# A new order of 594 steps, with other engines, buffers and held stores, for a fused attention and adapter kernel

## The chip, the core and the metric

The kernel runs on one core of a Trainium2 chip. The time is that of the device, in microseconds; a lower one is better. The core has five engines that work side by side, each through its own instructions in a fixed order: TensorE (PE, matrix products; PEld is its loading of weights), VectorE (DVE), ScalarE (ACT), GpSimd (POOL) and SyncE (SP). An instruction that needs another engine's result, or a buffer that another engine still uses, waits on a semaphore, and all that is queued behind it on its engine waits too. Transfers between HBM and the core's memory are issued here by POOL and SP, and run on 16 DMA engines.

## What is computed

Two layers, one after the other. The first is an attention without softmax (8 batches, 8 heads, 576 positions, 64 values per head), the second a mixture of two out of eight small adapters on each of the 4608 rows:

```python
q_p, k_p = phi(q, cos_w, sin_w), phi(k, cos_w, sin_w)   # relu(x) * cos, relu(x) * sin
kv = np.einsum('bhsf,bhsd->bhfd', k_p, v)
z = np.sum(k_p, axis=2)
num = np.einsum('bhsf,bhfd->bhsd', q_p, kv)
den = np.einsum('bhsf,bhf->bhs', q_p, z)[..., None] + 1e-06
x = num / den                                           # rows of 512
logits = x @ w_gate
# for the two largest logits of a row: softmax weight w, expert e
delta += w * ((x @ A[e]) @ B[e])
out = x + delta
```

## The kernel before

**Batches and groups.** Each batch's 576 positions lie as 64 partitions times 9 columns j. K, V and Q of a batch are loaded by POOL, which also casts them to bf16 on the way (lines 399, 401 and 419; the first K halves come through SP, line 410, into two output buffers). For each batch K goes through a ReLU (lines 432 on ACT, 434 on DVE) and V is scaled by the cosine and the sine of the position: on DVE as one product for four or two heads' pairs (line 446), on ACT as nine activations, one for each j (line 444). PE forms the state of a batch in 72 or 2 x 36 small matmuls (line 457, "kv"), which DVE or ACT copies into a block matrix BD (lines 469 and 471).

The output rows are made in 36 groups of 128 rows. Groups of kind "one" take two columns of one batch, groups of kind "two" take one column of two batches; the last nine groups all need batches 6 and 7. For a group PE transposes Q (line 541), ACT applies the ReLU (line 547), DVE multiplies by the tangent (line 567), PE multiplies with the state (line 585, "num"), and DVE takes the reciprocal of the denominator (line 596) and the quotient, xt (line 601). PE transposes xt (line 610), ACT or DVE copies it (xT, lines 245 and 247), and PE multiplies with the adapters' A and the gate together (line 623, "za").

Router steps go by 13 keys of three groups each (the last two of two and one): two largest logits, their sum, difference, mask, sigmoid, weights and weighted z (lines 637 to 672), a transpose on PE (line 681) and its copy (zgT). The output of a group is the product with B, with or without xt added on PE through the identity (lines 692 and 694, "dx"), then either a copy by ACT (line 245) or an addition of xt by DVE (line 704) into an output buffer, osb. Each key's three groups share one of seven osb buffers, which are written out by SP or POOL (lines 714 and 717).

**What sets the order.** Every step is declared with `pl.add`: its engine or alternatives, what it needs and makes, the buffers that it uses. Three tables at the top of the file, made outside of it by a search, then decide: `ORDER` is the one order in which all 594 steps are issued, and so the order on each engine; `CHOICE` says which alternative (engine) a step takes; `SLOTS` which buffer each use of a pool gets. In `Plan.run` nothing is computed any more, the tables are checked and the steps returned in order. Semaphores follow from the data and the buffers.

Two short tables are beside them. `HOLD` maps a store to another issue that has to come first: the store then waits for that issue, on its own queue. `FILL` puts a number of matmuls without use (line 318, 252 columns each) ahead of a step on PE, whose result is overwritten.

```python
            if s.idx in fill:
                pe_fill(fill[s.idx], s)
            issued[s.idx] = s.emit()
            if s.idx in hold:
                tc.add_manual_dep(issued[s.idx].ins, issued[hold[s.idx]].ins.name,
```

At the start DVE clears four BD matrices (line 331) and sets a matrix of ones, warm (line 299), on which PE runs 2 x 18 wide matmuls (line 305) while loads arrive; POOL makes a ramp TVi (line 257), ACT its sine and cosine TVf (lines 260 and 261, the second with the constant halfpi as bias), and DVE and PE spread the tangents into TT by way of the identity (lines 271, 275, 282 and 289).

Of the kernel before, what the change touches and what calls it, by code (L numbers as in the profile page):

```python
# [17 lines left out]


ORDER = [  # L20
    26, 0, 1, 19, 27, 29, 17, 20, 14, 45, 2, 16, 9, 23, 15, 13, 36, 10, 32, 11, 12, 28, 33, 18, 3, 37, 31, 4, 46, 51,
    7, 21, 8, 48, 30, 52, 38, 50, 39, 49, 35, 44, 41, 34, 115, 61, 114, 5, 62, 40, 116, 42, 22, 6, 43, 117, 118, 55,
    60, 121, 54, 70, 125, 122, 124, 119, 120, 126, 135, 71, 123, 145, 134, 127, 144, 136, 298, 154, 69, 131, 53, 137,
    299, 128, 132, 300, 79, 146, 129, 130, 155, 147, 57, 47, 156, 301, 133, 56, 80, 65, 302, 58, 59, 303, 138, 64,
    141, 78, 170, 171, 139, 142, 140, 161, 172, 160, 143, 24, 148, 162, 25, 305, 304, 149, 151, 173, 306, 355, 163,
    373, 152, 356, 150, 63, 88, 153, 307, 157, 357, 360, 358, 374, 308, 158, 375, 359, 159, 309, 66, 378, 361, 73, 89,
    310, 68, 67, 362, 74, 363, 167, 164, 87, 364, 181, 168, 165, 180, 376, 166, 190, 377, 182, 191, 169, 311, 174,
    312, 183, 313, 177, 175, 379, 97, 192, 176, 393, 178, 72, 314, 200, 315, 394, 75, 193, 201, 395, 398, 396, 179,
    412, 397, 96, 76, 380, 77, 316, 399, 83, 381, 82, 187, 184, 188, 400, 107, 185, 413, 206, 186, 207, 417, 189, 194,
    317, 202, 208, 414, 197, 195, 415, 196, 416, 106, 81, 382, 216, 217, 318, 369, 98, 209, 84, 198, 218, 418, 419,  # L30
    365, 370, 219, 387, 86, 199, 320, 366, 385, 105, 92, 85, 383, 386, 210, 384, 91, 319, 203, 388, 321, 322, 401,
    204, 211, 226, 390, 205, 227, 402, 430, 212, 228, 323, 431, 213, 324, 229, 236, 237, 435, 432, 214, 403, 433, 238,
    90, 392, 223, 215, 367, 404, 405, 239, 434, 368, 420, 93, 436, 224, 421, 437, 406, 101, 372, 326, 94, 325, 407,
    95, 450, 100, 327, 220, 408, 246, 221, 422, 451, 247, 410, 222, 424, 423, 438, 225, 230, 439, 99, 329, 328, 442,
    455, 452, 330, 248, 102, 453, 231, 425, 411, 443, 232, 454, 469, 103, 456, 457, 104, 440, 233, 470, 441, 444, 426,
    234, 474, 471, 445, 447, 235, 249, 427, 472, 458, 110, 332, 473, 459, 331, 240, 333, 464, 475, 241, 250, 476, 460,
    465, 242, 273, 429, 272, 461, 292, 109, 274, 462, 253, 252, 243, 254, 463, 477, 409, 275, 282, 478, 283, 468, 467,
    244, 263, 293, 255, 334, 466, 284, 262, 245, 487, 251, 264, 335, 481, 488, 371, 108, 336, 448, 337, 489, 265, 111,
    428, 338, 490, 492, 449, 285, 491, 482, 483, 493, 113, 294, 479, 494, 507, 112, 480, 484, 495, 256, 508, 496, 486,
    485, 509, 512, 259, 257, 510, 258, 511, 499, 501, 513, 260, 514, 500, 266, 261, 502, 497, 339, 267, 506, 515, 268,  # L40
    340, 516, 269, 505, 498, 341, 342, 517, 270, 504, 343, 276, 271, 526, 277, 518, 279, 278, 344, 521, 446, 280, 527,
    345, 281, 286, 346, 391, 531, 528, 347, 529, 287, 289, 288, 530, 348, 519, 532, 503, 522, 290, 543, 533, 520, 525,
    291, 534, 295, 523, 544, 535, 524, 349, 545, 389, 548, 546, 351, 350, 547, 536, 352, 549, 296, 540, 550, 537, 560,
    297, 541, 538, 561, 551, 562, 353, 565, 539, 552, 563, 354, 555, 564, 542, 566, 553, 567, 557, 556, 554, 568, 579,
    558, 569, 570, 580, 571, 559, 581, 589, 584, 582, 574, 573, 583, 575, 572, 585, 586, 576, 577, 587, 588, 578, 590,
    591, 592, 593,
]
CHOICE = [
    0, 0, 0, 0, 0, 0, 0, 0, 0, 0, 0, 0, 0, 0, 0, 0, 0, 0, 0, 0, 0, 0, 0, 0, 0, 0, 0, 0, 0, 0, 0, 0, 0, 0, 0, 0, 0, 0,
    0, 0, 0, 0, 1, 0, 0, 0, 0, 1, 1, 1, 0, 0, 0, 1, 0, 0, 0, 0, 0, 0, 0, 0, 0, 1, 0, 0, 0, 0, 0, 0, 0, 0, 0, 0, 0, 0,  # L50
    0, 0, 0, 0, 0, 0, 1, 0, 0, 0, 0, 0, 0, 0, 0, 0, 0, 0, 0, 0, 0, 0, 0, 0, 0, 0, 0, 0, 0, 0, 0, 0, 0, 0, 0, 0, 0, 0,
    0, 0, 0, 0, 0, 0, 0, 0, 0, 0, 0, 0, 0, 0, 0, 0, 0, 0, 0, 0, 0, 0, 0, 0, 0, 0, 0, 0, 0, 0, 0, 0, 0, 0, 0, 0, 0, 0,
    0, 0, 0, 0, 0, 0, 0, 0, 0, 0, 0, 0, 0, 0, 0, 0, 0, 0, 0, 0, 0, 0, 0, 0, 0, 0, 0, 0, 0, 0, 0, 0, 0, 0, 0, 0, 0, 0,
    0, 0, 0, 0, 0, 0, 0, 0, 0, 0, 0, 0, 0, 0, 0, 0, 0, 0, 0, 0, 0, 0, 0, 0, 0, 0, 0, 0, 0, 0, 0, 0, 0, 0, 0, 0, 0, 0,
    0, 0, 0, 0, 0, 0, 0, 0, 0, 0, 0, 0, 0, 0, 0, 0, 0, 0, 0, 0, 0, 0, 0, 0, 0, 0, 0, 0, 0, 0, 0, 0, 0, 0, 0, 0, 0, 0,
    0, 0, 0, 0, 0, 0, 0, 0, 0, 0, 0, 0, 0, 0, 0, 0, 0, 0, 0, 0, 0, 0, 0, 0, 0, 0, 0, 0, 0, 0, 0, 0, 0, 0, 1, 0, 0, 1,
    0, 0, 0, 0, 0, 0, 0, 0, 0, 0, 0, 0, 0, 0, 0, 0, 0, 0, 0, 0, 0, 0, 0, 0, 0, 0, 0, 0, 0, 0, 0, 0, 0, 0, 0, 0, 0, 0,
    0, 1, 0, 0, 0, 0, 0, 0, 1, 0, 0, 0, 1, 0, 0, 0, 0, 0, 0, 0, 0, 0, 1, 0, 0, 0, 0, 0, 0, 0, 1, 0, 0, 0, 0, 0, 0, 0,
    0, 0, 0, 0, 0, 0, 0, 0, 0, 0, 1, 0, 1, 0, 0, 0, 0, 0, 0, 0, 0, 0, 0, 0, 0, 0, 0, 0, 0, 0, 1, 1, 0, 0, 0, 0, 0, 0,
    0, 0, 0, 0, 0, 0, 1, 1, 0, 0, 0, 1, 0, 0, 0, 0, 0, 0, 0, 0, 0, 0, 1, 1, 0, 0, 0, 0, 0, 1, 0, 0, 0, 0, 0, 0, 0, 0,  # L60
    0, 0, 0, 0, 0, 0, 1, 1, 0, 0, 0, 0, 1, 0, 0, 0, 0, 0, 0, 0, 0, 0, 0, 1, 1, 0, 0, 0, 0, 0, 1, 0, 0, 0, 0, 0, 0, 0,
    0, 0, 0, 1, 1, 0, 0, 0, 0, 0, 1, 0, 0, 0, 0, 0, 0, 0, 0, 0, 0, 0, 0, 1, 1, 0, 0, 0, 0, 0, 1, 1, 0, 0, 0, 0, 0, 0,
    0, 0, 0, 0, 0, 0, 0, 0, 0, 0, 0, 0, 0, 0, 0, 0, 0, 0, 0, 0, 1, 1, 1, 0, 0, 0, 0, 0, 0, 0, 0, 0, 0, 0, 0, 0, 0, 1,
    0, 0, 0, 0, 0, 0, 0, 0, 0, 0, 0, 0, 0, 0, 0, 0, 0, 0, 1, 0, 0, 1, 1, 0,
]
SLOTS = [
    0, 1, 0, 2, 0, 1, 0, 1, 0, 1, 0, 0, 1, 0, 1, 0, 0, 1, 2, 2, 2, 2, 0, 2, 3, 3, 3, 1, 0, 3, 0, 1, 4, 0, 0, 0, 1, 0,
    0, 2, 0, 1, 2, 2, 2, 1, 1, 2, 3, 3, 1, 0, 0, 3, 3, 0, 1, 1, 0, 0, 0, 1, 1, 1, 0, 1, 2, 1, 2, 3, 2, 2, 1, 0, 4, 0,
    1, 5, 3, 3, 1, 2, 6, 0, 0, 7, 1, 4, 1, 1, 8, 3, 1, 0, 0, 9, 1, 2, 10, 0, 0, 0, 1, 11, 1, 0, 12, 2, 2, 0, 1, 13, 1,
    2, 14, 3, 3, 0, 0, 15, 1, 1, 2, 3, 4, 0, 2, 0, 1, 1, 1, 0, 4, 0, 1, 3, 1, 0, 0, 0, 5, 1, 2, 6, 2, 2, 0, 1, 1, 0,  # L70
    0, 7, 3, 3, 0, 2, 8, 0, 0, 9, 3, 4, 1, 1, 10, 2, 2, 1, 2, 13, 0, 0, 12, 2, 3, 1, 1, 14, 0, 2, 11, 3, 1, 1, 0, 0,
    0, 1, 15, 1, 4, 1, 2, 2, 0, 0, 3, 0, 0, 1, 1, 4, 0, 0, 2, 1, 1, 2, 3, 3, 1, 0, 2, 1, 3, 2, 1, 3, 0, 0, 0, 1, 0, 2,
    3, 0, 3, 3, 2, 1, 1, 0, 3, 2, 1, 1, 2, 3, 0, 0, 1, 2, 0, 1, 2, 0, 0, 0, 3, 0, 3, 2, 0, 0, 0, 1, 1, 1, 0, 1, 3, 3,
    0, 2, 1, 0, 0, 0, 3, 1, 2, 4, 3, 2, 2, 1, 1, 1, 2, 0, 0, 5, 2, 1, 1, 0, 0, 0, 3, 1, 2, 6, 3, 3, 1, 1, 1, 1, 2, 1,
    2, 0, 1, 1, 0, 0, 0, 0, 3, 0, 2, 1, 1, 3, 0, 1, 1, 1, 0, 1, 0, 4, 2, 3, 1, 0, 0, 0, 2, 0, 2, 2, 1, 3, 0, 1, 1, 1,
    3, 1, 3, 0, 2, 0, 2, 0, 0, 0, 3, 0, 2, 5, 3, 0, 1, 1, 1, 1, 1, 1, 2, 1, 0, 3, 0, 0, 0, 2, 0, 1, 6,
]

HOLD = [
    (371, 392), (409, 98), (446, 486), (503, 504),  # L80
]

FILL = [
    (7, 2), (118, 13), (135, 2), (56, 2), (138, 8),
]


# [780 lines left out]
```

## Time and profile before

| | us |
|---|---|
| three runs: median (lowest to highest) | 108.25 (108.07 to 109.98) |
| the profiled execution: its own time | 108.82 |
| its span, first to last instruction | 106.7 |

The busy time of an engine is the sum over its instructions, whatever they wait for in between. The page's groups show the costliest work:

| line | engine, what | count | busy us, mean ns |
|---|---|---|---|
| L585 | PE, num | 384 | 22.6, 223 |
| L601 | DVE, quotient xt | 36 | 24.0, 683 |
| L446 | DVE, V scaling | 17 | 18.9, 1138 |
| L547 | ACT, ReLU of transposed Q | 20 | 18.4, 944 |
| L245 | ACT, copies into osb | 29 | 15.6, 567 |
| L245 | ACT, copies into xT | 16 | 14.9, 941 |
| L567 | DVE, tangent product | 20 | 12.3, 624 |
| L444 | ACT, V scaling, one j each | 27 | 9.1, 425 |

Loads come in at a steady rate: in the trace each load of 1.2 MB (576 KB as bf16) lands 2.8 to 2.9 us after the one before, and the last, K of batch 7, at 73.4 us. SP's first store is issued at 72.79 us; POOL's first at 55.42, behind the loads on the same queue. How matmuls overlap with one another is modelled in the profile, so that "PE busy" is not PE at its peak, and an idle engine costs nothing where another one sets the end.

### The profile page before, as it was taken

What the parts mean: (1) busy time and instruction counts of PE and PEld (TensorE: products, weight loads), DVE (VectorE), ACT (ScalarE), POOL (GpSimd) and SP (SyncE); (2) the same over time, 40 slices, a digit from 0 to 9 for tenths busy, and PEclk for the clock granted to TensorE, in tenths of its full rate; (3) what the DMA queues carried; (4) which work ended last, traced back from release to release, by engine and by line L of the source; (5) the groups of instructions that cost most, each with busy time, mean ns of one, the idle gap of its engine ahead of it and who ended that gap; (6) DMA issues with size and microseconds to landing.
All of it is one profiled execution on the core that took longest, in us unless ns stands there. A gap on an engine that the chain in (4) does not pass through costs nothing.

```text
span 106.7 us, 4019 instructions
## 1 busy us (share of the span) xinstructions
PE 90.9 (85%) x1693; PEld 66.7 (63%) x1704; DVE 89.9 (84%) x254; ACT 77.8 (73%) x139; POOL 33.3 (31%) x53
## 2 busy tenths in 40 slices
PE   4978999959788599976999999998979969998920
PEld 1334468847687589864768686874868657775300
DVE  5973819897999999999798998997999969989940
ACT  7406982996388749999999998968999732677620
POOL 6999965522402222226321121221200202040000
PEclk9999999999999999999999999999999999999995
DMA  2999999999999999999999999999999998888993
GB/s 79 357 179 204 192 198 207 207 210 194 203 208 209 206 208 208 208 207 210 206 213 203 207 213 203 207 208 285 395 331 269 220 292 266 274 217 256 381 390 131
DMA packets 18321, 24.70 MB, mean 231 GB/s; under 512 B 4256, under 2 KB 15648, under 8 KB 18304
## 3 DMA queue, kind: packets, MB, share of 16 engines
q0 software_dynamic: 15984, 16.98, 88.5%
q1 hardware_dynamic: 2320, 7.47, 21.2%
q8 instruction: 13, 0.21, 0.7%
q14 instruction: 4, 0.03, 0.1%
HBM read 28.85 MB, written 9.44 MB: 359 GB/s over the span
## 4 chain that ended last, share of the span: by engine, by line
PE 44%; DVE 27%; ACT 12%; issue 7%; POOL 5%; DVEq 0%; POOLq 0%
PE pnd L585 13%; DVE xt L601 7%; PE ps L610 6%; PE ps L623 5%; PE pnd L457 5%; DVE VV L446 4%; PE ps L305 4%; ACT VV L444 3%; PE ps L692 3%; PE ps L541 3%; ACT BD L469 3%; ACT qTcs L547 2%; DVE osb L704 2%; PE ps L694 2%; DVE qTcs L567 2%
## 5 line engine op out<-in xcount | busy, mean ns | idle before, releaser
L585 PE MATMUL pnd<-BD,qTcs 128*128 128x130 bf16 (+1 forms) x384 | 22.6, 223 | 2.7 <-issue 1.3
L601 DVE TENSOR_TENSOR xt<-pnd,rden 128x512 bf16<-128x512 f32 x36 | 24.0, 683 | 0.1
L585 PEld LDWEIGHTS <-qTcs 128*128 128x128 bf16 (+1 forms) x384 | 18.3, 103 | 6.1 <-issue 4.2
L547 ACT ACTIVATE qTcs<-ps 128x1024 bf16<-128x1024 bf16 (+1 forms) x20 | 18.4, 944 | 3.9 <-PE ps L541 3.7
L446 DVE TENSOR_TENSOR VV<-Vb,TV 128x2304 bf16<-128x2304 bf16 (+1 forms) x17 | 18.9, 1138 | 2.6 <-DMA Vb<-in_v_dram 2.6
L245 ACT COPY osb<-ps 128x512 f32<-128x512 f32 (+1 forms) x29 | 15.6, 567 | 3.8 <-DVE osb L247 1.5
L245 ACT COPY xT<-ps 128x1024 bf16<-128x1024 bf16 (+1 forms) x16 | 14.9, 941 | 4.5 <-PE ps L610 4.4
L610 PE MATMUL ps<-ident,xt 128*128 128x128 bf16 x144 | 13.5, 222 | 0.8 <-DVE xt L601 0.4
L567 DVE TENSOR_TENSOR qTcs<-qTcs,TT 128x1024 bf16<-128x1024 bf16 (+1 forms) x20 | 12.3, 624 | 1.2 <-ACT qTcs L547 1.2
L717 POOL DMA_DIRECT2D out_dram<-osb x9 | 4.9, 540 | 25.3 <-DVE ps L655 6.8
L541 PE MATMUL ps<-ident,Qb 128*64 128x128 bf16 x288 | 11.1, 221 | 1.5 <-ACT qTcs L547 1.0
L457 PE MATMUL pnd<-VV,Kb 64*64 64x130 bf16 x576 | 10.3, 218 | 1.6 <-DVE xt L601 1.2
L610 PEld LDWEIGHTS <-xt 128*128 128x128 bf16 x144 | 9.8, 115 | 3.1 <-DVE xt L601 0.8
L457 PEld LDWEIGHTS <-Kb 64*64 64x64 bf16 x576 | 8.8, 106 | 4.3 <-issue 2.3
L692 PE MATMUL ps<-xt,ident 128*128 128x512 bf16 x29 | 10.9, 381 | 0.6 <-DVE zgT L247 0.3
L305 PE MATMUL ps<-warm 128*128 128x512 bf16 x36 | 9.8, 435 | 1.5 <-DVE warm L299 1.5
L541 PEld LDWEIGHTS <-Qb 128*64 128x64 bf16 x288 | 8.7, 109 | 3.7 <-issue 2.3
L623 PE MATMUL ps<-AW,xT 128*128 128x136 bf16 x144 | 10.5, 223 | 0.1
L469 ACT CAST BD<-pnd 64x520 bf16<-64x520 f32 x15 | 9.0, 598 | 2.1 <-PE pnd L457 1.2
L623 PEld LDWEIGHTS <-xT 128*128 128x128 bf16 x144 | 9.0, 98 | 1.5
L694 PE MATMUL ps<-Ball,zgT 128*128 128x512 bf16 x25 | 9.2, 380 | 0.6 <-DVE zgT L247 0.6
L444 ACT ACTIVATE VV<-Vb,TVf 128x128 bf16<-128x128 bf16 (+1 forms) x27 | 9.1, 425 | 0.0
(63 smaller groups left out, 117.3 us busy)
## 6 DMA issues: line engine op xcount, KB each, us to landing
Vb<-in_v_dram POOLq DMA_DIRECT2D x6, 576.0 KB, 20.0
Qb<-in_q_dram POOLq DMA_DIRECT2D x6, 576.0 KB, 20.1
Kb<-in_k_dram POOLq DMA_DIRECT2D x6, 576.0 KB, 20.1
out_dram<-osb SPq DMA_DIRECT2D x10, 256.0 KB, 5.9
out_dram<-osb POOLq DMA_DIRECT2D x6, 256.0 KB, 10.1
out_dram<-osb SPq DMA_DIRECT2D x2, 768.0 KB, 3.4
osb<-in_k_dram SPq DMA_DIRECT2D x2, 576.0 KB, 4.1
Vb<-in_v_dram POOLq DMA_DIRECT2D x4, 288.0 KB, 6.7
```

What stands on the lines that cost most here:

```text
L245: nc.scalar.copy(o, i)
L305: nc.tensor.matmul(out=pF(up), lhsT=warm[:, 0:128], rhs=warm, start=True, stop=True)
L446: nc.vector.tensor_tensor(out=o, in0=i, in1=TV[:, cs].unsqueeze(1).to_broadcast([128, n, J, D]), op=ALU.mult)
L457: nc.tensor.matmul(out=pt[64 * hh:64 * hh + 64, par, a * 2 * W:(a + 1) * 2 * W], lhsT=kt[r, 2 * a + hh, j, :], rhs=vt[r, 2 * a + hh, j, :] ...
L541: nc.tensor.transpose(out=pt[64 * hh:64 * hh + 64, n, 2 * a:2 * a + 2, x], in_=qt[:, c, j, :], identity=ident)
L547: nc.scalar.activation(tQT[S_(uqt)][:, 0, 0:n], pB(up)[:, 0:n], AF.Relu)
L567: nc.vector.tensor_tensor(out=v[1], in0=v[0], in1=f4, op=ALU.mult)
L585: nc.tensor.matmul(out=nd[r, a, 0:4 * W].rearrange("p (h e w) -> p h e w", h=2, e=2)[:, :, par], lhsT=st, rhs=bd[:, par, a, cs].rearrange( ...
L601: nc.vector.tensor_tensor(out=tXT[S_(uxt)].rearrange("p (a h d) -> p a h d", a=2, h=4), in0=nd_view(und)[:, :, :, 0:D], in1=tRD[S_(urd)].u ...
L610: nc.tensor.transpose(out=pB(up)[:, lo:lo + 128], in_=tXT[S_(uxt)].rearrange("p (x c) -> p c x", c=4)[:, c], identity=ident)
L623: nc.tensor.matmul(out=pF(uza)[:, n * AW_W:(n + 1) * AW_W], lhsT=tXTT[S_(u)][:, k, c, :], rhs=AW[:, c, :], start=(c == 0), stop=(c == 3))
L692: nc.tensor.matmul(out=pF(udx), lhsT=ident, rhs=tXT[S_(uxt)], start=True, stop=False)
```

## The change

Only the five tables change. No step is added or dropped except fillers, and no function is touched.

- `ORDER`: almost every step has another place; neighbours on an engine mostly keep close to one another.
- `CHOICE`: 31 steps change. From DVE to ACT: V scaling of a half of batch 0 (the sine), of a half of batch 1 and of all of batch 2 (cosine), the copy of A and the gate (AW), zgT of keys 0 and 11, two output additions of "dx", two one-group copies of xT, two of the half-row copies at the end, and one half of batch 0's state. From ACT to DVE: V scaling of a half of batch 1, one K half's ReLU of batch 1, the halves of the states of batches 0 and 7, one two-group and one one-group copy of xT, zgT of key 3, one output addition. With an output copy that goes to ACT, PE adds xt through the identity, and with one that goes to DVE it doesn't. Five stores go from POOL to SP and two from SP to POOL.
- `SLOTS`: other buffers, for osb among others: keys 7 to 12 used buffers 4, 2, 0, 5, 1, 6 and now use 5, 1, 6, 2, 5, 3.
- `HOLD`: five stores wait for another issue instead of four.
- `FILL`: 24 fillers instead of 27, in other places.

On POOL's queue a load of Q (three columns of batch 0) and one of V now stand ahead of the ramp, the second half of V of batch 1 two places earlier, and V of batch 7 ahead of Q of batches 6 and 7. On DVE the four clears of BD and the warm matrix now stand ahead of halfpi.

```diff
--- before.py
+++ after.py
@@ -18,70 +18,70 @@
 ORDER = [
-    26, 0, 1, 19, 27, 29, 17, 20, 14, 45, 2, 16, 9, 23, 15, 13, 36, 10, 32, 11, 12, 28, 33, 18, 3, 37, 31, 4, 46, 51,
...
-    591, 592, 593,
+    26, 15, 31, 27, 14, 45, 19, 16, 20, 1, 17, 29, 0, 2, 36, 9, 3, 32, 11, 13, 33, 28, 10, 18, 51, 37, 30, 12, 4, 46,
...
+    592, 593,
 ]
...
 HOLD = [
-    (371, 392), (409, 98), (446, 486), (503, 504),
+    (371, 372), (390, 486), (391, 447), (429, 107), (467, 506),
 ]
 
 FILL = [
-    (7, 2), (118, 13), (135, 2), (56, 2), (138, 8),
+    (118, 7), (134, 2), (138, 7), (304, 8),
 ]
```

The numbers are those of the steps. In `HOLD` 371, 390, 391, 429 and 467 are stores by SP of keys 0, 1, 1, 3 and 5; 372, 486, 447 and 506 are stores by POOL of keys 0, 6, 4 and 7, and 107 is the load of Q of batch 7.

## The prediction

> **What bounds the kernel now.** I read the page's busy row first, then the windows cut at the starts of the state matmuls (kv, L457), then the chain of waits, then the DMA answers.
>
> ```profile
> PE 90.9 (85%) x1693; PEld 66.7 (63%) x1704; DVE 89.9 (84%) x254; ACT 77.8 (73%) x139; POOL 33.3 (31%) x53
> ```
>
> No engine alone fills the span of 106.7 us. The windows say where each is full (stretch, length, busy time of each engine, granted TensorE clock, DMA share, GB/s):
>
> ```profile
> 0.00:20.00 20.00, 17.59 (x209) 9.84 (x209) 13.51 (x30) 11.71 (x29) 15.93 (x27) 1.00 1.13 202
> 20.00:34.30 14.30, 11.86 (x248) 10.01 (x242) 12.81 (x35) 10.88 (x12) 4.31 (x7) 1.00 1.28 205
> 34.30:60.80 26.50, 23.39 (x530) 18.97 (x531) 25.31 (x69) 23.89 (x41) 7.58 (x10) 1.00 1.21 208
> 60.80:80.00 19.20, 17.94 (x382) 13.80 (x388) 17.99 (x50) 17.19 (x30) 3.31 (x6) 1.00 1.15 261
> 80.00:104.00 24.00, 20.12 (x340) 14.08 (x345) 20.31 (x75) 14.10 (x31) 2.19 (x4) 1.00 0.90 285
> ```
>
> The columns are PE, PEld, DVE, ACT, POOL. From 34.3 to 60.8 us DVE is busy 25.31 of 26.50: this middle is DVE's. Before it, DVE has 7.98 us of idle time (20 - 13.51 and 14.3 - 12.81); from 80 to 104 both DVE and PE have nearly 4 us. The cuts at 34.3, 60.8 and 80 are the starts of the state matmuls of batches 2, 5 and 7, "kv2", "kv5", "kv7" below.
>
> Loads do not bind. In the trace the K loads of batches 2, 5 and 7 land at 30.0, 56.3 and 73.4 us, 4.3, 4.5 and 6.5 us before their kv starts (of which the ReLU takes 0.75 on DVE or 2.1 on ACT).
>
> The chain of waits, in order of time, from kv7 on (start, length, what):
>
> ```profile
> 79.94 1.25 PE pnd L457 x69
> ...
> 84.84 0.53 PE pnd L585 x14
> 85.37 0.96 issue
> 86.33 0.25 PE pnd L585 x2
> ...
> 95.20 0.36 PE ps L610 x4
> ...
> 95.59 0.42 DVE xT L247
> ...
> 100.60 0.44 DVE osb L247
> ...
> 101.74 0.14 DVE osb L247
> ...
> 102.78 0.44 DVE osb L247
> 103.23 0.37 ACT osb L245
> ```
>
> From 79.94 to 95.6 the chain is PE, with one hole of 0.96 us in which PE waits for nothing the profile shows. From 95.6 it is a DVE-led ladder of router steps and copies. The hole is instruction fetch, as I read it:
>
> ```profile
> PEld L585 <- issue: 4.2, 9, 1.1
> ...
> q8 instruction: 13, 0.21, 0.7%
> ```
>
> Queue q8 moved 13 blocks of 16 KB, each in 0.9 to 1.0 us; the one from 84.52 to 85.44 ends inside the hole, the one from 72.26 to 73.20 lies by another (0.34 at 72.32). The chain's issue pieces after 70 us that are worth counting are 0.34, 0.18, 0.96, 0.15 and 0.28: 1.9 us.
>
> **The change, part by part.** Every step's computation is kept. I count each stage's steps in both orders and price them with rows: halves of V scaling 0.70 on DVE, 2.68 on ACT (9 of the 18 that took 5.36); a whole one 1.31 (half of 2.62) or 3.65; xt 0.60 and rden 0.12 back to back; state copy 0.69 on DVE, 0.60 on ACT; K ReLU 0.75, 2.1, halves 1.17 on ACT and about 0.4 on DVE (estimate: half of 0.75); two-group copy of xT 0.66 or 1.0, one-group 0.42 or 0.59; output copy 0.65 or 0.55, halves 0.42 or 0.37; sig 0.22, zgT 0.35 or 0.48. Small router steps and PE steps are alike in both orders.
>
> - Up to kv2: one half and one whole V scaling, and the copy of the adapter weights (0.28 + 0.17 on DVE, about 0.8 on ACT), go from DVE to ACT; a K half goes back, as does one xT copy. DVE -1.3, ACT +5.0, PE +0.2.
> - kv2 to kv5: DVE -0.1, ACT 0, PE -0.2, though within it kv4 stands later on PE, behind six output products (dx) where it was behind one.
> - kv5 to kv7: two more qT products on DVE, one residual add fewer; five more output copies on ACT. DVE +0.8, ACT 0, PE +0.5.
> - After kv7: DVE does 4 output copies where it did 7, one tan product, one xT and one zgT copy fewer. DVE -2.1, ACT +1.7, PE -0.4.
>
> Now what reaches the end. **To kv2** ACT decides. Walked by rows, ACT's work from its first table copy at 8.82 to the end of batch 2's ReLU is 0.21 + 3 x 2.68 + 0.57 + 6 x 1.0 + 0.6 + 1.17 + 3 x 0.6 + 3.65 + 0.8 + 2.1 = 24.9, so 33.8 without a gap; back-to-back pieces overlap by about 0.07 each, which gives near 33.0, against 33.93 now. Inputs are there in time: the second half of V of batch 1 is moved ahead of two loads on POOL's queue and lands near 14 instead of 15.57; V2, landed at 23.51, stays in place. At the start POOL issues a Q and a V load (0.92 + 0.72) before the ramp, so TVf comes 1.6 later, but it is then behind DVE's five memsets (four of 0.54, one of 0.48) and needs halfpi, now last of them; the tangent matmul waits for the identity, 7.44 now, 0.2 later then. I take 0 to there and -0.4 at kv2. **kv2 to kv5** 0. **kv5 to kv7**: DVE's +0.8 falls into a stretch with 1.2 us of DVE idle (19.2 - 17.99); I take +0.3. **After kv7** PE's -0.4 counts, since PE is the chain to 95.6; of the fetch hole of 0.96 I take half, -0.5; on the last ladder one 256-column copy (0.42) and one zgT copy leave DVE, and the last two copies run on ACT one behind the other, where now DVE's 0.44 is followed by ACT's 0.37: -0.7. Sum: -0.4 + 0 + 0.3 - 0.4 - 0.5 - 0.7 = -1.7.
>
> **Stores.** Three stores go from POOL to SP (SP 19 to 22, POOL 12 to 9). POOL's are cheap to drop: it idles up to 6.8 us for them. On SP one issue takes 1.16 us at the median, so its queue is 3.5 us longer; its last store before the final four goes at 94.9, the first of the four at 98.2, so 3.3 us of cover. The last needs only its own data; cost 0, at most 0.3. Every output buffer was followed to its next writer: the nearest is the buffer of router group 3, whose second store now stands fourth on SP (about 76, landed by 82) before group 7 writes it near 85. Cover 3 us; price if late, the lateness. The holds order stores behind other issues on one queue or the other and hold no engine but SP.
>
> **Fillers** fall from 27 to 24 matmuls of 0.12 (1.57 for 13). The granted clock is 1.00 in every window above. The Trainium skill, "TensorE: Matmul & The Clock Gate" (Why this matters for your kernels), speaks against fewer: a gap of some 3 us sends the clock back to half. By it one such window, 3.4 us at half speed, would cost 1.7 us. But from 20.0 to 34.3 PE idles 2.44 in all and the fillers there (10 x 0.12 = 1.2) would make 3.6, spread over 14 us; the longest single PE gap is 1.2. I take 0.
>
> A second rule of the skill speaks against the change's worth: "Runtime: NRT & Kernel Launch" (Instruction fetch mechanics), has the cost of a new 16 KB block "mostly hidden". By it the holes are not fetch and the store order buys nothing: the sum would be -1.2. By the row it is -1.7, and the bound of what fetch can give is the 1.9 above; that it costs more with SP's longer queue bounds it below, about +1.0 (one more such hole). I stay with the trace, at half of the one hole.
>
> **Rivals.**
> - *Nothing arrives.* DVE's relief after kv7 turns into DVE waiting for PE, which is the chain there and loses 0.4; the fetch hole moves. For it: PE 20.12 of 24 against DVE 20.31, so PE stays. Sum +0.3 - 0.4 - 0.2 = -0.3: median 108.0.
> - *All of it arrives.* DVE's -1.3 before kv2 and -2.1 after kv7 count whole, with 1.5 of the 1.9 of fetch: -1.3 + 0.3 - 2.1 - 1.5 = -4.6: 103.7. Against it: ACT ties the first, PE the second.
> - *ACT becomes the bound before kv2*, slower. ACT now has gaps of 0.80, 1.76, 0.82, 1.92 and 0.52 between 8.82 and 33.93, 5.8 in all. If 4 of them come back beside the 5.0 of new work, kv2 starts at 38.3, and the DVE-bound middle has 1.2 us of slack to take it in: +4.0, less the 1.6 after kv7: +2.4, median 110.7. It decides from kv2 near 38 on. Against it: the old gaps waited for qT transposes and state matmuls that now stand as early or earlier.
> - *It doesn't do what it says*: fetch holes as many as before. That is the first rival's -0.3, or my sum without its -0.5, 107.05.
>
> **The numbers.** The sum is against the profiled execution, 108.82 (span 106.7 and 2.1 around it): 107.1. The three timed runs have median 108.25, 0.57 less: 106.5. The forecast (105.4 to 107.4) has 0.42, nothing arrives (107.4 to 109) 0.23, all arrives 0.15, ACT 0.20. 2% is 2.17 us, about what a measurement of this kernel can tell from no change (its runs spread over 1.9). Faster by over 2% is below 106.1: two fifths of the forecast, 0.17, and all of the second, 0.15: 0.32. Slower is ACT's 0.20; the rest 0.48. Range: 104.2 leaves out half of the case of -4.6, 110.7 half of ACT's.
>
> **What would show it.** kv2 at 33.5 to 34.3 (right) or over 37 (ACT rival); kv7 within 1 us of 79.9; DVE busy near 87 and ACT near 84; from kv7 to the last copy 22 us where it is 23.7 now; issue pieces on the chain after 70 us near 1.4. I am wrong if PE waits on a store, if a Q transpose waits for ACT in the first 34 us, or if PE's clock falls below 1.00 before 100 us.

## The result, and the profile after

| | before | after |
|---|---|---|
| median, lowest to highest, us | 108.16 (108.03 to 109.98, 4 runs) | 106.66 (106.36 to 106.86, 4 runs) |
| profiled execution, its span | 108.82, 106.72 | 106.86, 105.09 |

The ratio is 0.986, interval 0.983 to 0.990: 1.4% less time, inside the 2% that count as no change, and 0.2 us from the predicted 106.5. Executions over 1.5% above the fastest of the same kernel are left out of all ratios here; most of the kernels have some, and the one without fillers has four of ten, at 109.4 to 109.8 us and a mean granted clock of 0.961 to 0.964.

The busy row of the changed kernel, first part of the page:

```profile
PE 91.4 (87%) x1692; PEld 67.0 (64%) x1702; DVE 89.2 (85%) x248; ACT 82.9 (79%) x161; POOL 31.1 (30%) x50
```

ACT took over 5.1 us of work, DVE shed only 0.7, and PE grew by 0.5: none of the three that fill the stages got shorter by what the kernel gained. So the time is again read by stages. The windows of the changed kernel, cut at its own kv2, kv5, kv7 and just short of the end of the copies at 100.88 (stretch, length, then PE, PEld, DVE, ACT, POOL, granted clock, DMA share, GB/s):

```profile
0.00:20.00 20.00, 17.40 (x193) 9.11 (x194) 13.27 (x28) 12.97 (x33) 15.80 (x27) 1.00 1.15 205
20.00:34.46 14.46, 12.70 (x260) 10.81 (x260) 13.88 (x37) 14.18 (x27) 4.25 (x6) 1.00 1.28 204
34.46:60.34 25.88, 23.28 (x537) 19.10 (x539) 25.16 (x69) 23.19 (x42) 7.26 (x10) 1.00 1.21 208
60.34:79.24 18.90, 18.00 (x361) 13.73 (x363) 18.76 (x51) 16.94 (x31) 1.64 (x3) 1.00 1.16 268
79.24:100.70 21.46, 20.00 (x348) 14.23 (x350) 18.16 (x68) 15.39 (x34) 2.17 (x4) 1.00 0.91 287
```

ACT is now full ahead of kv2, 14.18 of 14.46, and DVE full from 60.34 to 79.24, 18.76 of 18.90. The stages themselves, from the instructions' own times (the last packet is the last piece of a store to move):

| stage, us | before | after | difference |
|---|---|---|---|
| start to kv2 | 34.32 | 34.46 | +0.14 |
| kv2 to kv5 | 26.47 | 25.88 | -0.59 |
| kv5 to kv7 | 19.15 | 18.90 | -0.25 |
| kv7 to end of last output copy | 23.67 | 21.64 | -2.03 |
| last copy to last packet | 1.65 | 2.96 | +1.31 |
| last packet to end of span | 1.46 | 1.25 | -0.21 |

These make -1.63; another -0.33 lies outside the span. Two rows carry the story: the last stage gained two microseconds, and then the stores took 1.3 back.

One execution is not the kernel, and the first row shows it. Six other profiles of the changed order, in kernels that leave the work ahead of kv2 as it is (one but for its fillers), have kv2 at 33.90, 33.90, 33.91, 33.98, 34.24 and 34.72 us; four of the old order with its choices have it at 34.30 to 34.36. In the changed order kv2 follows ACT's first table copy (TT) by 24.82 or 24.83 us each time; what varies is that copy, from 9.06 to 9.89. It waits for PE, which runs through its first 18 warming matmuls before. These take 0.63 us each at first and 0.38 later, and that turn came at 7.7 us in the profile above and at 5.1 in that of the stores put back (below). The granted clock stands at 1.00 all the while, so the row doesn't say why.

The chain of waits of the changed kernel in its last stage, from kv7 on (start, length, what):

```profile
79.31 1.18 PE pnd L457 x69
...
84.20 0.59 PE pnd L585 x16
84.79 0.35 PE ps L610 x4
85.14 0.17 PE ps L681 x3
85.31 0.60 PE pnd L585 x16
...
93.23 3.92 DMA out_dram<-osb
97.15 0.67 DVE osb L704
...
99.12 0.41 DVE osb L247
99.53 0.23 DVE zgT L247
99.76 0.05 issue
99.81 0.40 PE ps L694
100.23 0.37 ACT osb L245
100.61 0.27 ACTq L863
```

The 0.96 us of "issue" that stood at 85.37 has no successor. The ladder at the end is shorter by the DVE copy that ACT now takes. And there is a new line: a store of 3.92 us ahead of a DVE addition at 97.15, into the buffer that this store has just written out. It is no wait. DVE's own timeline has no gap there:

```profile
96.80 0.42 DVE L672 TENSOR_TENSOR zg<-ps,w 128x256 bf16<-128x256 f32 x1
97.14 0.68 DVE L704 TENSOR_TENSOR osb<-ps,xt 128x512 f32<-128x512 f32 x1
```

The chain goes back to the last event that a step could have waited for, and the landing of the store came as DVE got free. In the profile without holds the same addition comes as early, counted from kv7 (17.9 us in both), with no store in its chain.

### The profile page after: what moved, and what is told of

It is laid out like the page before. It is cut to its first block, busy times and chain, and to the rows that moved or that the text cites. A ratio compares the mean times of both kernels' runs of the same rounds, so it can differ in the third digit from the quotient of the medians.

```text
span 105.1 us, 4032 instructions
## 1 busy us (share of the span) xinstructions
PE 91.4 (87%) x1692; PEld 67.0 (64%) x1702; DVE 89.2 (85%) x248; ACT 82.9 (79%) x161; POOL 31.1 (30%) x50
## 4 chain that ended last, share of the span: by engine, by line
PE 46%; ACT 21%; DVE 18%; issue 5%; DMA 4%; ACTq 0%; SPq 0%; DVEq 0%
PE pnd L585 13%; PE ps L305 10%; ACT qTcs L547 7%; PE pnd L457 6%; PE ps L610 5%; ACT BD L469 4%; PE ps L541 4%; DVE xt L601 4%; DMA out_dram<-osb 4%; PE ps L623 3%; ACT Kb L432 3%; ACT VV L444 2%; ACT xT L245 2%; DVE VV L446 2%; ACT osb L245 2%
## 5 line engine op out<-in xcount | busy, mean ns | idle before, releaser
L585 PE MATMUL pnd<-BD,qTcs 128*64 128x130 bf16 (+1 forms) x384 | 22.5, 222 | 2.5 <-ACT BD L469 1.7
L585 PEld LDWEIGHTS <-qTcs 128*64 128x64 bf16 (+1 forms) x384 | 18.2, 103 | 5.7 <-issue 3.0
L446 DVE TENSOR_TENSOR VV<-Vb,TV 128x2304 bf16<-128x2304 bf16 (+1 forms) x15 | 17.0, 1155 | 3.3 <-DMA Vb<-in_v_dram 3.3
L245 ACT COPY osb<-ps 128x512 f32<-128x512 f32 (+1 forms) x32 | 16.5, 564 | 2.1 <-PE ps L694 1.0
L444 ACT ACTIVATE VV<-Vb,TVf 128x128 bf16<-128x128 bf16 (+1 forms) x45 | 15.5, 432 | 0.0
L305 PE MATMUL ps<-warm 128*128 128x512 bf16 x36 | 10.7, 467 | 2.6 <-DVE warm L299 2.6
L541 PE MATMUL ps<-ident,Qb 128*64 128x128 bf16 x288 | 11.7, 222 | 0.8 <-issue 0.7
L717 POOL DMA_DIRECT2D out_dram<-osb x7 | 3.8, 537 | 26.4 <-ACT sig L662 10.7
L469 ACT CAST BD<-pnd 64x520 bf16<-64x520 f32 x14 | 8.4, 600 | 1.9 <-DVE BD L471 1.6
```

Source lines behind the costliest of these rows:

```text
L245: nc.scalar.copy(o, i)
L305: nc.tensor.matmul(out=pF(up), lhsT=warm[:, 0:128], rhs=warm, start=True, stop=True)
L444: nc.scalar.activation(o[:, :, j], i[:, :, j], AF.Copy, scale=TVf[:, cs, j:j + 1])
L446: nc.vector.tensor_tensor(out=o, in0=i, in1=TV[:, cs].unsqueeze(1).to_broadcast([128, n, J, D]), op=ALU.mult)
L469: nc.scalar.copy(o, i)
L541: nc.tensor.transpose(out=pt[64 * hh:64 * hh + 64, n, 2 * a:2 * a + 2, x], in_=qt[:, c, j, :], identity=ident)
```

## Experiments

### The choices without the order, and the order without the choices

The kernel before with only the changed `CHOICE`:

```diff
 CHOICE = [
-    0, 0, 0, 0, 0, 0, 0, 0, 0, 0, 0, 0, 0, 0, 0, 0, 0, 0, 0, 0, 0, 0, 0, 0, 0, 0, 0, 0, 0, 0, 0, 0, 0, 0, 0, 0, 0, 0,
+    0, 0, 0, 0, 0, 0, 0, 0, 0, 0, 0, 0, 0, 0, 0, 0, 0, 0, 0, 0, 0, 0, 0, 0, 0, 1, 0, 0, 0, 0, 0, 0, 0, 0, 0, 0, 0, 0,
...
```

> The kernel before with the new engine choices only (order, buffers, holds and fillers as before). If the gain is the relief of VectorE, which the choices make, it is here: ratio to before 0.986 to 0.990. If order and choices only pay together, since ScalarE's extra 5 us ahead of batch 2's state matmul then stand where nothing was cleared for them: 1.00 to 1.02, with that matmul starting after 36 us instead of 34.3.

Measured: 112.2 us, ratio 1.037 (1.033 to 1.041), worse than either case expected. kv2 starts at 39.01. The timeline of this kernel on ACT (start, length, what, tiles; in brackets the idle time before it and what ended it):

```profile
27.46 1.21 ACT L469 CAST BD<-pnd 64x520 bf16<-64x520 f32 x2 [1.82 <-PE pnd L457]
28.70 3.70 ACT L444 ACTIVATE VV<-Vb,TVf 128x256 bf16<-128x256 bf16 x9
32.42 1.94 ACT L547 ACTIVATE qTcs<-ps 128x1024 bf16<-128x1024 bf16 x2
34.25 0.62 ACT L245 COPY AW<-Ald 128x512 bf16<-128x512 bf16 x1
34.76 0.23 ACT L245 COPY AW<-Gld 128x32 bf16<-128x32 bf16 x1
34.88 2.13 ACT L432 ACTIVATE Kb<-Kb 128x2304 bf16<-128x2304 bf16 x1
```

From 27.46 to 37.0 ACT has no gap. The whole V scaling of batch 2 and two ReLUs of Q stand ahead of the copy of the adapter weights (AW), and PE waits for that copy 2.6 us, from 32.44:

```profile
35.04 2.88 PE L623 MATMUL ps<-AW,xT 128*128 128x136 bf16 x24 [2.60 <-ACT AW L245]
```

This is the slower rival of the prediction (kv2 at 38.3), in the kernel that has the moved work but not the order. Part of the lateness is the clock, which was at 0.50 from 34.38 to 37.79: those 24 matmuls took 2.88 us, where 12 take 0.82 on the chain of the changed kernel, so by estimate 1.2 us of it.

The changed kernel with the old `CHOICE`:

```diff
 CHOICE = [
-    0, 0, 0, 0, 0, 0, 0, 0, 0, 0, 0, 0, 0, 0, 0, 0, 0, 0, 0, 0, 0, 0, 0, 0, 0, 1, 0, 0, 0, 0, 0, 0, 0, 0, 0, 0, 0, 0,
+    0, 0, 0, 0, 0, 0, 0, 0, 0, 0, 0, 0, 0, 0, 0, 0, 0, 0, 0, 0, 0, 0, 0, 0, 0, 0, 0, 0, 0, 0, 0, 0, 0, 0, 0, 0, 0, 0,
...
```

> The changed kernel with the engine choices of before (order, buffers, holds and fillers as changed). If the choices carry the gain: ratio to before 1.00 to 1.01. If the order carries it: 0.985 to 0.990. If they only pay together: 1.00 or more here too.

Measured: 109.09 us, ratio 1.007 (1.004 to 1.010). kv2 starts at 36.16 and the last stage takes 22.3 us (its profile is of an execution of 110.87 us, with the clock at 0.50 from 38.7 to 42.1, behind kv2). Alone, the two halves cost 3.7% and 0.7%; together they gain 1.4%. A sum of part prices cannot give that. The likely reading is that the order opens on ACT the room that the choices fill: up to kv2 ACT is here busy 22.7 of 36.2 us, in the changed kernel 27.2 of 34.5.

### The holds

The changed kernel with `HOLD = []`:

```diff
-HOLD = [
-    (371, 372), (390, 486), (391, 447), (429, 107), (467, 506),
-]
+HOLD = []
```

> The changed kernel without its five holds, so that stores go as soon as their data and their queue allow. If the holds keep fetch and the last stores free of traffic, it is slower than the changed kernel: ratio to before 0.99 to 1.00, with new holes of 0.5 to 1 us on TensorE after 70 us. If the holds are idle: 0.986, no new hole.

Measured: 106.85 us, ratio 0.987 (0.983 to 0.991), that of the changed kernel; kv7 to last copy 21.64, to the hundredth the same. The holds do nothing for the time that this comparison, good to some 0.4%, could show.

### Storing the last groups earlier

If the last stores set the end, part of their data could leave sooner. The stores of keys 9 and 10 are cut into one for each group, behind its own copy:

```diff
+    LATE = (542, 559)
+    SPLIT = {}
+    for key, steps in ((9, (537, 539, 541)), (10, (554, 556, 558))):
+        for i, n in enumerate(steps):
+            g = seq[3 * key + i]
+            SPLIT[n] = (g, 1, 0, i, ("OSB", key), "SP")
...
+            if s.idx in LATE:
+                continue
             issued[s.idx] = s.emit()
...
+            if s.idx in SPLIT:
+                store(*SPLIT[s.idx])()
```

> The changed kernel with the store of each of router groups 9 and 10 cut into three, each issued behind its own output copy instead of behind the third. If the last 7 us are bound by the bandwidth of the last four stores (2.4 MB), as the full DMA rows from 97 to 103 us suggest, they start about 1 us earlier and the end comes 0.4 to 1.0 us earlier: ratio to before 0.977 to 0.983. If the ladder of router steps and copies that the chain of waits shows is the bound, nothing changes: 0.986; if the shorter packets cost more than the earlier start gives: 0.987 to 0.992.

Measured: 107.27 us, ratio 0.992 (0.989 to 0.995), not better than the changed kernel and nearest to the third case expected. In its profile the last copy ends at 100.42 and the last packet at 103.30, a distance of 2.88. From 96 to 98 us the DMA engines of the changed kernel are already busy 0.88 of the time, with the stores before these, so there was little room to start in. No version that writes the whole output beat the changed kernel.

### The queues of the stores

The changed kernel with its seven moved stores back on their old queues, no holds:

```diff
 CHOICE = [
...
-    0, 0, 0, 1, 1, 0, 0, 0, 0, 0, 0, 0, 1, 0, 0, 0, 0, 0, 0, 0, 0, 0, 0, 0, 0, 0, 0, 0, 0, 0, 0, 1, 0, 0, 0, 0, 0, 0,
+    0, 0, 0, 1, 1, 0, 0, 0, 0, 0, 1, 0, 1, 0, 0, 0, 0, 0, 0, 0, 0, 0, 0, 0, 0, 0, 0, 0, 0, 0, 1, 1, 0, 0, 0, 0, 0, 0,
...
```

> The changed kernel with its seven re-assigned stores on the queues that they had before (five go back from SP to POOL, two from SP's list to... the other way round, so POOL has 12 and SP 19), and no holds. Order and all other choices stay those of after. If the queue of a store is what held up fetch, the 0.96 us hole near 83 to 86 us comes back, or fetch blocks start later after their crossing (over 3 us for the last three instead of 0.45 to 1.5), and the ratio to before is 0.990 to 0.998. If the queues are idle for the time, as the holds were, the ratio is that of after, 0.984 to 0.988, with kv7 within 0.4 us of 79.2.

Measured: 107.23 us, ratio 0.989 (0.984 to 0.993), between the two cases. The profile decides: the late hole does not come back, the last three fetches start 0.66, 1.22 and 0.90 us after their block crossing, and kv7 to last copy is 21.65. What this execution lost lies elsewhere: kv2 to kv5 took 27.32 instead of 25.88. The windows show why. In the changed kernel:

```profile
36.00:38.00 2.00, 0.99 (x16) 0.92 (x15) 2.00 (x4) 1.32 (x3) 0.28 (x1) 1.00 1.21 208
38.00:40.00 2.00, 2.00 (x49) 1.80 (x47) 1.97 (x7) 0.99 (x2) 0.46 (x1) 1.00 1.21 208
```

and with the stores back (the eighth number is the granted clock):

```profile
36.00:38.00 2.00, 1.53 (x15) 1.53 (x15) 1.95 (x5) 0.78 (x2) 0.33 (x1) 0.55 1.22 212
38.00:40.00 2.00, 2.00 (x37) 1.71 (x36) 1.71 (x4) 0.11 (x1) 0.41 (x1) 0.59 1.20 203
```

PE looks busier and does less, 37 matmuls instead of 49 in the second stretch; ACT, which waits for it, idles. So the hole's absence is not owed to the queues of these stores, as far as one profile tells; the clock is taken up below.

### The moved work ahead of kv2

The changed kernel with four choices of the early part back on DVE:

```diff
 CHOICE = [
...
-    0, 1, 0, 0, 0, 1, 0, 0, 0, 0, 1, 0, 0, 0, 0, 1, 0, 1, 0, 0, 0, 0, 0, 0, 0, 1, 1, 0, 0, 0, 0, 0, 0, 0, 0, 0, 0, 0,
+    0, 0, 0, 0, 0, 1, 0, 0, 0, 0, 1, 0, 0, 0, 0, 1, 0, 0, 0, 0, 0, 0, 0, 0, 0, 1, 0, 0, 0, 0, 0, 0, 0, 0, 0, 0, 0, 0,
...
```

> The changed kernel with four choices before kv2 back where they were: the copy of the adapter weights, the two pieces of V scaling and the K ReLU piece that had moved from DVE to ACT are on DVE again. ACT was busy 14.18 of 14.46 us between 20 us and kv2. If ACT bounds this stretch, kv2 comes 0.5 to 1.5 us earlier than 34.46 and the ratio falls below 0.982. If the order has been fitted so that both are at their bound, DVE gets 1.3 to 2.5 us more work there with 1.7 us of idle time left, and kv2 stands at 34.5 to 36 with the ratio at 0.986 to 1.000. I expect the second.

The four steps are the copy of the adapter weights and three pieces of V scaling (half of batch 0, half of batch 1, all of batch 2); no K ReLU is among them, other than the expectation has it. Measured: 107.73 us, ratio 0.995 (0.992 to 0.999); kv2 at 35.32. The stretch from 20 us to it:

```profile
20.00:35.32 15.32, 12.95 (x259) 10.74 (x258) 14.41 (x37) 8.30 (x9) 4.40 (x7) 1.00 1.28 205
```

ACT, relieved, is busy 8.30 of 15.32 us and has one gap of 5.14; DVE, with 14.41, is now nearly as full as ACT was. So ACT was filled in the changed kernel up to DVE's pace and not beyond: less work on ACT made kv2 later, 26.13 us behind the first table copy instead of 24.83.

### Are the last stores bound by bandwidth?

First with half of the partitions of the last four stores left out (the other half of those rows is not written):

```diff
         def f():
             if kind == "two":
+                if b == 7:
+                    o = out[(b - 1) * S:(b + 1) * S].rearrange("(p j) d -> p j d", j=J)[0:64, x:x + n]
+                    return q_.dma_start(out=o, in_=tOSB[S_(uo)][0:64, i:i + n])
```

> The changed kernel with the last four stores (768, 768, 512 and 256 KB) each writing only their first 64 of 128 partitions: half of their 2.36 MB is left out, everything else is computed. If the bandwidth of these stores sets the end in the changed kernel, the last packet comes 1.0 to 1.4 us earlier (near 102.5 us for a last copy at 100.9, that is 1.65 us behind it as in the kernel before) and the ratio to before falls to 0.973 to 0.978. If the ladder of copies sets the end and the last store's fixed latency follows it, the end moves by less than 0.4 us, ratio 0.983 to 0.987.

> The kernel before with the same half of its last four stores left out. There the last packet ended 1.65 us after the last copy, so the store's fixed latency and not the bandwidth should set the end: ratio 0.996 to 1.000. If bandwidth set the end there too, it falls by as much as in the changed kernel, to 0.987 to 0.990. The difference of the two half-store kernels is what the ladder of the changed order would be worth without the stores: 2.5 us or more if bandwidth hid it, 1.5 us if it hid nothing.

Measured: 0.984 (0.979 to 0.989) and 1.000 (0.995 to 1.005). Half of the bytes are gone and nothing is gained, which at first sight refutes the bandwidth theory. The windows of the half-store version of the changed kernel say otherwise:

```profile
98.00:100.00 2.00, 1.67 (x8) 0.40 (x5) 1.56 (x9) 1.65 (x6) 0.00 (x0) 1.00 0.89 227
100.00:102.00 2.00, 0.39 (x1) 0.10 (x1) 0.02 (x1) 0.86 (x3) 0.00 (x0) 1.00 0.96 207
```

beside the same stretches of the changed kernel:

```profile
98.00:100.00 2.00, 1.66 (x7) 0.40 (x5) 1.35 (x7) 1.58 (x6) 0.00 (x0) 1.00 0.99 409
100.00:102.00 2.00, 0.20 (x1) 0.00 (x0) 0.00 (x0) 0.65 (x2) 0.00 (x0) 1.00 1.02 423
```

The last two numbers are the DMA engines' share and the rate. In both kernels the engines are full from 100 to 102 us, but from 64 partitions they move 207 GB/s, from 128 partitions 423. In that stretch one packet of 6 KB took 0.46 us on the mean, instead of 0.23. The cut had halved the bytes and the rate together, so it tested nothing. The next pair keeps all partitions and shortens what each of them stores, to the first group of each store, 1.0 MB instead of 2.36 (the other groups are not written):

```diff
...
+                if b == 7:
+                    n_ = 1
+                    o = out[(b - 1) * S:(b + 1) * S].rearrange("(p j) d -> p j d", j=J)[:, x:x + n_]
+                    return q_.dma_start(out=o, in_=tOSB[S_(uo)][:, i:i + n_])
...
```

> The changed kernel with each of the last four stores cut to the first of its row groups, all 128 partitions kept: 256 KB each in 2 KB packets, 1.0 MB instead of 2.36 (1.3 MB of the output is left out). Halving the partitions made each packet take twice as long (0.41 us for 6 KB instead of 0.24) and so left the store time as it was; here the bytes of each partition fall. If the stores' bandwidth sets the end of the changed kernel, the last packet follows the last copy by 1.5 to 2.0 us instead of 2.96 and the ratio to before is 0.972 to 0.979. If a fixed latency does, the distance stays over 2.6 us and the ratio at 0.984 to 0.988.

> The kernel before with the same cut of its last four stores. Its profile had 1.65 us between last copy and last packet, with one fetch hole of 0.96 us before; another execution of the same order had no such hole, came to the last copy 1.3 us earlier and ended at the same time. If bandwidth sets the end in executions without the hole, the ratio is 0.987 to 0.995 and the spread between executions is larger than before; if bandwidth never binds in it, 0.998 to 1.002. Set against the changed kernel with the same cut, the gain of the change without its stores should be 1.8 to 2.5 us under the bandwidth theory, 1.5 us or less under the other.

Measured: 105.96 us, ratio 0.977 (0.971 to 0.983), and 108.17 us, ratio 0.996 (0.992 to 1.000). In the first, last copy to last packet takes 1.65 us instead of 2.96, though the copy itself was late in that execution by a half clock. The last stretches:

```profile
98.00:100.00 2.00, 1.93 (x13) 0.76 (x11) 1.56 (x8) 1.67 (x6) 0.00 (x0) 1.00 0.69 246
100.00:102.00 2.00, 0.74 (x3) 0.19 (x2) 0.64 (x3) 1.39 (x5) 0.00 (x0) 1.00 0.49 188
```

The engines are no longer full. The whole, split and half stores of the changed order left 2.56 to 3.45 us between last copy and last packet, in seven profiles. So bandwidth does set the end of the changed kernel, and 1.65 us is what a last store takes when little is queued ahead of it: the kernel before had 1.65 as well, and has it with its last stores whole but the 27 earlier ones left out (the next experiment). In times the same shows less clearly: without the bulk of the last stores the change is worth 1.9% (0.977 over 0.996), with it 1.4%, and the intervals overlap. How much of the gain the stores hide is not settled by them.

### Do stores hold up instruction fetch?

The kernel before without the 27 stores of keys 0 to 8 (their rows are not written) and without holds:

```diff
         q_ = nc.sync if eng == "SP" else nc.gpsimd
 
         def f():
+            if b != 7:
+                return None
```

> The kernel before without its 27 stores of router groups 0 to 8 (three quarters of the output is left out, everything is computed, the last four stores stay; no holds). If the packets of queued stores are what a fetch of instructions waits for, fetches after 65 us start within 1.5 us of their block crossing instead of 2.9 to 4.5, the holes near 46, 72 and 85 us are gone or below 0.2, and the ratio is 0.978 to 0.988 (up to 1.9 us of holes, and the last stores find an empty queue). If fetch does not depend on stores, the lags stay at 2.9 to 4.5 us and the ratio is over 0.993.

Measured: 107.23 us, ratio 0.990 (0.986 to 0.994), a little short of what was expected. The table follows one fetch, that of the eleventh block of PE's instructions. A crossing is where PE goes over to the next 256 instructions; the time of a fetch is that of its packets on queue q8.

| kernel | crossing at | fetch starts after, us | KB moved meanwhile | PE's hole at the next crossing |
|---|---|---|---|---|
| before | 80.14 | 3.75 | 938 | 0.96 |
| before, half partitions in the last stores | 80.00 | 2.57 | 610 | none |
| before, last stores cut | 79.97 | 4.09 | 990 | 1.21 |
| before, 27 stores left out | 79.99 | 0.82 | 0 | none |
| changed | 79.51 | 1.31 | 360 | none |
| changed, stores on the old queues | 80.41 | 0.66 | 142 | none |

The crossings are counted from PE's records, of which a few can be missing, and the KB are little more than the rate times the delay. The first three kernels do the same work up to that time. So the hole is a matter of chance in the old order, present in two of three executions, and goes with how late the fetch starts. With no stores about, the fetch starts within a microsecond: stores do hold it up. In the changed order it starts 0.7 to 2.9 us after the crossing, and none of eight profiles has a gap over 0.2 us on PE from 80 to 95 us, with the stores on either queue, with holds and without them. So neither holds nor queues are what removed the hole; that it is the new order is likely, but the order was not changed in that place alone. By which road packets delay a fetch was not separated.

What the hole cost at the end is less than its length. In the old order with half partitions, without the hole, the last copy ends at 102.33 us instead of 103.61, but the last packet at 105.20 instead of 105.26 (those half stores take as long as whole ones: in the changed order 24.51 against 24.60 us from kv7 to the last packet). In these two profiles the stores hid it. With the 27 stores left out, the last copy ends at 102.33 too and the last packet at 103.98. So the 1% of this run is for the most part the emptier queue of the last stores, and not the fetch.

Nor are such holes gone. The fetch of the fifth block, among the loads, starts 2.8 us after its crossing in the kernel before and leaves a hole of 0.41 us at 46.06, off the chain, where ACT's V scaling leads. In the changed kernel it starts 3.9 us after it, and the hole stands on the chain:

```profile
46.25 0.75 issue
```

In the other six profiles of the changed order with its fillers and most of its choices it is 0.62 to 0.97 us.

### The fillers

The changed kernel with `FILL = []`:

```diff
-FILL = [
-    (118, 7), (134, 2), (138, 7), (304, 8),
-]
+FILL = []
```

> The changed kernel without its 24 filler matmuls (0.12 us each, they compute nothing that is read). If they keep the clock up, a window before 40 us shows a granted clock below 1.00 and the kernel is 1 to 3 us slower, ratio 0.996 or more. If PE's gaps are short enough without them, the clock stays at 1.00 and the ratio is that of the changed kernel, 0.983 to 0.988, or 0.2 lower where a filler stood on the path.

Measured: ratio 0.989 (0.985 to 0.994), which the changed kernel's overlaps. In the profiled execution the clock is at 1.00 in each window up to 101 us. That says less than it seems to: the clock falls in some executions only, and the mean granted clock of the six in the ratio reaches down to 0.968, where that of the six of the kernel without holds was 0.989 to 0.998. What fillers are worth stays open.

## Why the prediction was right, and where it was not

- **The time.** Sum on record -1.7, profiled execution -1.96; 106.5 against 106.66. The end is right, and in part by luck: to the last copy the kernel gained 2.73 us, and the distance to the last packet, which the sum left as it was, took 1.31 of it back.
- **To kv2, -0.4: measured +0.14 in the profiled execution, and -0.3 to -0.4 in four of the six others.** From the TT copy on, the term was about right: that copy to kv2 took 25.50 us before and 24.83 after, and ACT is what is full, as said. "I take 0 to there" is where the executions differ: the copy came 0.2 to 1.1 us later than its 8.82 before, 0.81 in the profiled one. The prediction let the tangent matmul wait for the identity alone, 0.2 later, which came true where the warming matmuls ahead of it on PE were done in time (copy at 9.06 to 9.08); in the other four profiles they were not. DVE got no relief here: its busy time up to kv2 rose by 0.8 where -1.3 was counted, since, among others, one more quotient (0.66) comes before kv2 and three small casts (line 326) take 0.5 longer. The rival (ACT bound, kv2 at 38.3) is what the choices give in the old order, with kv2 at 39.01, by estimate 1.2 of that by the clock. What the argument against it did not say is that the order is a condition for the choices.
- **"Loads do not bind" holds, but with less room.** The landing times given (30.0, 56.3 and 73.4 us) are not those of the trace, which has 31.4, 57.8 and 75.5. ACT's ReLU of K of batch 2 starts 0.4 us after its load has landed in the kernel before and 0.8 in the changed one, so that a faster ACT would soon find the load ahead of kv2.
- **kv2 to kv5, 0: measured -0.59,** but 27.3 us in the two profiles with a half clock. It was priced as DVE's stage, and DVE's busy time did fall by about as little as counted, 0.12; its idle time fell from 1.19 to 0.72 us, which no row of the profile before announces. Why is open.
- **kv5 to kv7, +0.3: measured -0.25** against the profiled execution, -0.1 against three others of the old order (19.0), and 18.9 to 19.1 in each later profile of the changed order with its choices. The +0.3 was too much: DVE's additional 0.8 went whole into the "stretch with 1.2 us of DVE idle".
- **After kv7, -1.6 in three terms: measured -2.03 to the last copy.** Of this the hole is 0.96, and not the half of it that was taken. An execution of the old order without the hole needs 22.53 from kv7 to the last copy against 21.64: PE's and the ladder's terms, on record as -1.1, are worth 0.9. To the last packet all three are worth 0.7 (25.32 against 24.60).
- **The step that was missing: the stores behind the last copy.** The prediction let the end follow the last copy at an unchanged distance, and gave the stores "cost 0, at most 0.3" for SP's longer queue. It looked at when stores are issued, not at how many bytes are under way: the distance grew by 1.31. The rate was on the page of before, up to 390 GB/s in the last slices.
- **Fetch.** That the holes are fetch fits the table. The two times given for q8 (84.52 to 85.44, 72.26 to 73.20) are not in the trace; the transfers before those holes end at 84.82 and 71.26, and PE goes on 1.5 and 1.4 us after each. "Ends inside the hole" was therefore wrong, and what convinces is the table above. The rule of the Trainium skill, "Runtime: NRT & Kernel Launch" (Instruction fetch mechanics), "mostly hidden", holds for most of the 13 blocks; at three of them the kernel before has a hole, of 0.41, 0.34 and 0.96 us.
- **Fillers, 0 against the 1.7 estimated by the rule.** Right for the profiled execution, at 1.00 up to the end of the copies. But the rule was set aside by the longest gap of 1.2, and the clock did fall to half in other executions of the changed order, after gaps of 0.93 and 1.04 us. That cost 1.44 us from kv2 to kv5 (27.32 against 25.88).
- **The stated signs.** ACT 82.9 for 84, kv7 within 1 us, last stage 21.64 for 22, issue pieces on the chain after 70 us worth counting 1.5 for 1.4 (0.87 of them ahead of an ACT copy at 75.57): as said. kv2 34.46 for 33.5 to 34.3: missed in this execution, met in five of six others. DVE 89.2 for 87: missed. Of the signs of being wrong, PE waits on no store, no Q transpose waits for ACT in the first 34 us, and the clock stays up in the profiled execution; it fell in two others.

## What to carry to other kernels

Cost the tail behind the last compute step by the bytes that are still under way at the DMA rate of the last slices, not by the issue of the last store: a faster ladder is worth little once the engines are full behind it. Do not add prices of engine choices and of an order as if they were independent; run each half alone. When an experiment halves a load, see in the windows that the rate did not halve with it. And read a stage from several executions before crediting a change with half a microsecond of it.

## What the runs showed of the hardware

- Stores from 64 partitions move at half the rate of stores from 128 with all 16 DMA engines full: 207 against 423 GB/s, 0.46 against 0.23 us for a packet of 6 KB (100 to 102 us, the last four stores halved against the changed kernel).
- A fetch of PE's next instruction block (0.9 to 1.0 us by itself) starts 0.3 to 0.8 us after a crossing when nothing else moves (27 stores left out, 11th and 12th block), and up to 4.4 us after it in the kernel before; where PE had stopped, it went on 1.4 to 1.5 us after the transfer had ended.
- The granted clock fell to 0.50 for 3.4 us in two profiled executions of the changed order (36.2 to 39.6 us with the stores back, 36.4 to 39.8 with the last stores cut), with no gap on PE over 1.1 us since the warming, and did not in four others with the same two gaps. The Trainium skill, "TensorE: Matmul & The Clock Gate" (Part 1), has the activity window free-running, which would make this a matter of phase; no run here shows that.
